# Masking the Gram matrices of a delta-rule attention on VectorE, straight out of PSUM, in a kernel for one Trainium2 core

## The chip, the cores and the metric

The kernel runs on one core of one Trainium2 chip. Its time is the device time of one execution in microseconds (us); the number given is the median of three runs. The engines are named as in the profile: PE (TensorE, matrix products; PEld is its loading of weights), DVE (VectorE), ACT (ScalarE), POOL (GpSimd), and SP (SyncE, which only issues DMAs here). PSUM is the memory that PE writes to; SBUF is the memory that all engines share.

## The reference

Three stages follow each other. First a delta-rule attention with batch 4, 8 heads, 768 tokens and head size 48, here per batch and head:

```
for t in range(S):
    y[t]  = q[t] @ state
    v_old = k_n[t] @ state                 # k_n: k over its norm
    state = state + beta[t] * outer(k_n[t], v[t] - v_old)
```

Its output, 3072 tokens of 384 values, goes through a mixture of 4 experts (`relu(x @ w1[e]) @ w2[e]`, 384 to 1024 to 384, weighted by normalized probabilities), and then through a gated layer (`sigmoid(x @ w_gate) * (x @ w_val) @ w_out`, 384 to 1536 to 384). All values are fp32.

## The kernel before

**Steps.** The token loop is cut into 12 steps of 64 tokens. A step handles all 32 pairs of batch and head: two halves of the batch lie on partitions 0 to 63 and 64 to 127, and an index i of 2 and 8 heads lie in the free dimension. Within a step the recurrence becomes matrix products: a Gram matrix of keys with keys gives L, which must be scaled by a weight per token (`w_all`, made of beta and the key norms) and inverted as a triangular system, and a Gram matrix of keys with queries gives P, which must be masked to be strictly triangular. From step 4 on, two steps share one inverse, and the six pairs of steps feed six blocks of 512 tokens to the two layers.

**Layers.** The layers are PE's main load. Each fp32 product is made of three fp32r products (high and low parts of both factors, `split3`). A unit of an expert has 9 matmuls up (`ph`, L689) and 9 down (`acc`, L726). Between them ScalarE writes the high part `hhi` of the activations (L696) and VectorE the low part `hlo`; the products down of a unit are emitted two units after the products up, those of the last three units of an expert one after the other. Weight tiles are split as they come: a ScalarE cast for the high part (`ws`, L190) and a VectorE subtraction for the low one. At an expert's end VectorE scales the three accumulators (`ctmp`) and GpSimd adds them to `ACC` (L753). VectorE's calls go through a counting wrapper and all show line 112 in the profile.

**Order.** It is written out by a planner when the kernel is built. `plan(t, fn, "pe")` gives a task a due time on PE's own account of work; `slot()` is called between the groups of layer matmuls and emits tasks that are due, one task with PE work at a time. Two lists of background work are filled in as VectorE's account (`vec_at`, which `vec.` calls raise) allows: the multiplies and subtractions of the inverse (`itmp`, `Xpp`, `Lpp`), and, until about 390 us, the decoding of the gated layer's weights (`dec_a`, `dec_b`, parts of `Xpp` and `Lpp` as buffers), which uses ScalarE, VectorE and two GpSimd products (L239, L240) each. Every engine runs its own list in order.

**The Gram matrices.** `plan_g` (L863) plans steps 4 to 11; steps 0 to 3 are done at the start. It loads keys and queries (`KQ`), copies keys into block-diagonal weights (`bdG`), and plans four tasks, one for each i and group of 4 heads. A task runs four matmuls into one PSUM bank `pg` (`g_mm`, L314; the profile counts eight), which holds 64 columns of L and 64 of P for each head. `g_raw` (L338) has ScalarE copy the bank to the tile `LP`. Nine units of due time after the first task, in one entry:

```
plan(t + 23, lambda: (scale_l(c), l_out(c), l_off(c), scale_p(c), p_out(c)))
```

`scale_l` (L347) and `scale_p` (L342) are GpSimd products over the whole step, 128x1024 each, in place in `LP`; `l_out` and `p_out` send L and P to DRAM by GpSimd's DMA queue (`ld`, `pd`), from where the inverse and the outputs read them back. `pg` is taken from the pool `at`, which has two banks in this part of the program and serves the attention's other tasks too.

Steps 0 and 1 do the same at the start with `g_l` (L321) and `g_p` (L330): VectorE multiplies the bank's L by the weights and its P by the mask and writes `LP`, 128x256 each.

Of the kernel before, what the change touches and what calls it, by code (L numbers as in the profile page):

```python
# [40 lines left out]
WARM0, WARM1 = 4, 14  # L41
DEC0, DEC1 = 7.0, 150.0
CH1, CH2, TR1, TR2 = 70.0, 42.0, 44.0, 16.0
# inverses: the steps that share one, and whether it stops at half chunks
INV = [((0,), True), ((1,), True), ((2, 3), True)]
INV += [((2 * k, 2 * k + 1), False) for k in range(2, NPAIR)]

# [25 lines left out]
AT2 = {k: n for n, k in enumerate(ORDER2)}  # L73
NG1, NG2 = len(ORDER1) // 2, len(ORDER2) // 2

# (kind, block, expert, first step of the block, number of steps)
EARLY = 1
PHASES = [("m1", 0, e, s, 1) for s in range(2) for e in range(EARLY)]
PHASES += [("m1", 0, e, 0, 2) for e in range(EARLY, NE)] + [("m2", 0, 0, 0, 2)]
# [5 lines left out]
def moe_delta_kernel(  # L85
# [13 lines left out]
):  # L99
    nc = tc.nc  # L100

    # what the tensor and vector engines have been given so far, in microseconds of their own work
    pe_at, vec_at = [0.0], [0.0]

    class Counted:
# [38 lines left out]
    KQi = [KQ[:, :, i] for i in range(2)]  # L144
    KS = ap_.tile([112, 2, H, C], F32, name="KS")
    bdG = ap_.tile([112, 2, H, P], F32, name="bdG")
# [15 lines left out]
    p_d = dr1.tile([NE, NT], F32, name="p_d")  # L162
    w2_d = dr1.tile([NG2, P, 2 * DM], F32, name="w2_d")

    # ------------------------------------------------------------ weights
    stream = []
    for kind, b, e, _, _ in PHASES:
        stream += [(kind, e * NG1 + g) for g in range(NG1)] if kind == "m1" else [(kind, g) for g in range(NG2)]
# [99 lines left out]
        items.sort(key=lambda r: r[0])  # L268
        back["dec"] += items

    # ------------------------------------------------------------ attention
    x_hi, x_lo = {}, {}
    x_done = set()
    ld_t, od_t, xd_t, pd_t = {}, {}, {}, {}
# [7 lines left out]
    def load_kq(c):  # L282
        (q[1] or q[0]).dma_start(out=KQ, in_=kq[c])
# [4 lines left out]
    def fill_bd(bd, t, i, eng):  # L288
        eng(out=bd[64:112, i, :, 0:C], in_=t[i][64:112, 0])
        eng(out=bd[0:48, i, :, C:P], in_=t[i][0:48, 0])  # L290
# [18 lines left out]
    def bank(shape, name):  # L309
        turn[0] += 1  # L310
        p, tag = free[turn[0] % len(free)]
        return p.tile(shape, F32, tag=tag, name=name)

    def g_mm(i, hg, bd, kq_t):  # L314
        pg = bank([P, 4, 2, C], "pg")
        for j in range(4):
            h = hg * 4 + j
            nc.tensor.matmul(out=pg[:, j], lhsT=bd[0:112, i, h], rhs=kq_t[i][0:112, :, h], start=True, stop=True)  # L318
        return pg

    def g_l(pg, c, i, hg):  # L321
        hs = slice(hg * 4, hg * 4 + 4)
        vec.tensor_tensor(
            out=Lts[c % 2][:, i, hs],
            in0=pg[:, :, 0],
            in1=w_all[:, 2 * c + i, hs].unsqueeze(2).to_broadcast([P, 4, C]),
            op=ALU.mult,
        )

    def g_p(pg, c, i, hg):  # L330
        vec.tensor_tensor(
            out=Pts[c % 2][:, i, hg * 4 : hg * 4 + 4],
            in0=pg[:, :, 1],
            in1=mask_sb.unsqueeze(1).to_broadcast([P, 4, C]),
            op=ALU.mult,
        )

    def g_raw(pg, c, i, hg):  # L338
        hs = slice(hg * 4, hg * 4 + 4)
        nc.scalar.copy(out=LP[c % 2][:, :, i, hs].rearrange("p a h t -> p h a t"), in_=pg)  # L340

    def scale_p(c):  # L342
        t = Pts[c % 2].rearrange("p i h t -> p (i h) t")
        m = mask_sb.unsqueeze(1).to_broadcast([P, 2 * H, C])
        nc.gpsimd.tensor_tensor(out=t, in0=t, in1=m, op=ALU.mult)

    def scale_l(c):  # L347
        t = Lts[c % 2].rearrange("p i h t -> p (i h) t")
        w = w_all[:, 2 * c : 2 * c + 2].rearrange("p i h -> p (i h)").unsqueeze(2).to_broadcast([P, 2 * H, C])
        nc.gpsimd.tensor_tensor(out=t, in0=t, in1=w, op=ALU.mult)  # L350

    def l_out(c):
        lt = Lts[c % 2]
        r, c2 = INV_OF[c]
        steps, small = INV[r]
        l_done.add(c)
        lv = [lt[o : o + HC].rearrange("p i h t -> p (i h) t") for o in range(0, P, HC)]
        if small:
            if c2 == 0:
                ld_t[r] = dr.tile([len(steps), 2, 2, H, 2, HC, HC], F32, tag=f"ls{len(steps)}", name="ls")  # L360
                od_t[r] = dr.tile([len(steps), 2, H, 2, HC, HC], F32, tag=f"lo{len(steps)}", name="lo")
            for a in range(2):
                for bp in range(2):
                    q[0].dma_start(
                        out=ld_t[r][c2, a, :, :, bp].rearrange("i h s t -> s (i h) t"),
                        in_=lv[2 * bp + a][:, :, a * HC : (a + 1) * HC],
                    )
            return
        if c2 == 0:
            ld_t[r] = dr.tile([len(steps), 2, H, 2, HC, 3 * HC], F32, tag="ld", name="ld")  # L370
        for bp in range(2):
            ld = ld_t[r][c2, :, :, bp]
            q[0].dma_start(out=ld[:, :, :, 0:C].rearrange("i h s t -> s (i h) t"), in_=lv[2 * bp])
            q[0].dma_start(
                out=ld[:, :, :, C:].rearrange("i h s t -> s (i h) t"), in_=lv[2 * bp + 1][:, :, HC:]
            )

    def l_off(c):
        lt = Lts[c % 2]
        r, c2 = INV_OF[c]  # L380
        if INV[r][1]:
            for bp in range(2):
                q[0].dma_start(
                    out=od_t[r][c2, :, :, bp].rearrange("i h s t -> s (i h) t"),
                    in_=lt[bp * C : bp * C + HC].rearrange("p i h t -> p (i h) t")[:, :, HC:],
                )

    def p_out(c):
        pd_t[c] = dr.tile([P, 2 * H * C], F32, tag=f"pd{c % 2}", name="pd")
        q[0].dma_start(out=pd_t[c], in_=Pts[c % 2].rearrange("p i h t -> p (i h t)"))  # L390
# [211 lines left out]
            rows += [[lambda i=i: s_task(c, i) for i in range(2)]] if c < NC - 1 else []  # L602
        return rows

    # ------------------------------------------------------------ norms
    nt_ = cp.tile([P, 3, 2 * NC, H], F32, name="norm_tmp")

    def norm_sum(t, c0, n):
# [47 lines left out]
        )  # L656
        nc.sync.dma_start(out=p_d.rearrange("e (g j) -> g e j", j=P), in_=d)

    # ------------------------------------------------------------ mixture
    acc_t, p_t = {}, {}  # L660

    def load_p(n):
# [95 lines left out]
                out=x_lo[b, 2][:, d, cols], in0=a, in1=xh.bitcast(F32), op=ALU.subtract  # L758
            )

    # ------------------------------------------------------------ schedule
    def unit_us(kind, ns):
        return (18 if kind == "m1" else 27) * (ns * STEP / 2.4e3 + 0.0025)

# [9 lines left out]
    def plan(t, fn, kind=""):  # L774
        todo.append((t, len(todo), kind, fn))
# [87 lines left out]
    def plan_g(c, t):  # L863
        plan(t, lambda: load_kq(c))
        for i in range(2):
            plan(t + 12, lambda i=i: fill_bd(bdG, KQi, i, nc.scalar.copy))
        for n, (i, hg) in enumerate([(0, 0), (0, 1), (1, 0), (1, 1)]):
            plan(t + 14 + 2 * n, lambda i=i, hg=hg: g_raw(g_mm(i, hg, bdG, KQi), c, i, hg), "pe")
        plan(t + 23, lambda: (scale_l(c), l_out(c), l_off(c), scale_p(c), p_out(c)))

    def startup():
        zero = pre_lo[:, 0]
# [145 lines left out]
    with tc.manual_schedule():  # L1018
# [11 lines left out]
        for c in range(4, NC, 2):  # L1030
            t = dec_mem[c // 2] if c < NC - 2 else dec_mem[2]
# [9 lines left out]
        for k in range(1, NPAIR):  # L1041
            w = W[k]
            if k > 1:
                r0 = max(M2[0] + 27.0, w - 270.0)
                plan_inv(k + 1, r0, r0 + 22.0, w - CH1 - 14.0)
            if k + 1 < NPAIR:
                plan_g(2 * k + 2, w - 161.0)
                plan_g(2 * k + 3, w - 135.0)
            plan_chain(2 * k, w - (CH1 if k > 1 else 70.0), 3.9)
            plan_chain(2 * k + 1, w - (CH2 if k > 1 else 34.0), 3.9)  # L1050
            plan_tr(2 * k, w - (TR1 if k > 1 else 22.0), 4.0)
            plan_tr(2 * k + 1, w - (TR2 if k > 1 else 8.0), 4.0)
# [100 lines left out]
```

## Time and profile before

| | |
|---|---|
| median of 3 runs | 1531.97 us (1531.19 to 1533.07) |
| the profiled execution: its span, first to last instruction | 1529.9 us; no other time of it is given |
| PE busy | 1473.9 us (96%) |
| PEld busy | 1224.4 us (80%) |
| DVE busy | 1089.4 us (71%) |
| ACT busy | 592.7 us (39%) |
| POOL busy | 303.4 us (20%) |
| mean granted PE clock | 0.978 of full speed |

The shares are means over stages with different limits. Up to about 100 us PE starts up; from 150 to 300 us VectorE is busy nearly all the time; from 300 us on PE is. Matmuls are pipelined, so the duration of a single one in a row (about 390 ns for 128x512) overlaps with the next. In rows of waits the engine on the left stood idle for the one on the right, and "idle before" belongs to the instruction behind it. The granted clock is a share of PE's full speed; 0.5 is its lower level, 1.2 GHz.

### The profile page before, as it was taken

How to read it: one execution, taken by the hardware profiler on the slowest of the kernel's cores; microseconds unless marked ns; L12 is line 12 of the kernel's file. 1: busy time of each engine (PE TensorE's matmuls, PEld its weight loads, DVE VectorE, ACT ScalarE, POOL GpSimd, SP SyncE). 2: the span in 40 equal slices, each digit the busy share in tenths (PEclk: the TensorE clock that was granted, in tenths of full speed). 3: DMA queues.
4: the chain of work that ended last, by engine and by line, in shares of the span. 5: the costliest groups of instructions: out<-in, count | busy, mean ns of one | idle time of the engine just before them, and what ended most of it. 6: DMA issues, size and time to landing. Idle time of an engine off the chain costs nothing. (4 is left out here: it accounts for less than half of the span.)

```text
span 1529.9 us, 23026 instructions
## 1 busy us (share of the span) xinstructions
PE 1473.9 (96%) x8801; PEld 1224.4 (80%) x8801; DVE 1089.4 (71%) x1841; ACT 592.7 (39%) x953; POOL 303.4 (20%) x309
## 2 busy tenths in 40 slices
PE   5899989999999999999999999999999999999998
PEld 5688767888887888887888887788888888888877
DVE  7877998846889866778756778766778754444553
ACT  4045554533343334344343444343433333433343
POOL 4241567530033210013210003220001120001100
PEclk8689999999999999999999999999999999999999
DMA  8586776675443584434485334494433462433221
GB/s 227 165 262 208 225 244 238 213 210 157 147 138 107 164 202 142 131 121 147 134 222 156 122 121 131 132 236 142 142 100 106 124 167 84 133 108 101 93 93 62
DMA packets 97749, 235.50 MB, mean 154 GB/s; under 512 B 23544, under 2 KB 29816, under 8 KB 95608
## 3 DMA queue, kind: packets, MB, share of 16 engines
q1 hardware_dynamic: 87352, 195.04, 41.2%
q0 software_dynamic: 10144, 38.94, 9.7%
q8 instruction: 69, 1.13, 0.3%
q14 instruction: 40, 0.33, 0.1%
q10 hardware_dynamic: 144, 0.07, 0.0%
HBM read 202.10 MB, written 27.97 MB: 150 GB/s over the span
## 5 line engine op out<-in xcount | busy, mean ns | idle before, releaser
L689 PE MATMUL ph<-xhi,ws 128*128 128x512 f32 (+1 forms) x2064 | 635.7, 390 | 1.5 <-ACT xhi L756 0.8
L726 PE MATMUL acc<-hhi,ws 128*128 128x512 f32 (+1 forms) x1632 | 499.0, 388 | 1.3 <-ACT hhi L696 1.3
L689 PEld LDWEIGHTS ph<-xhi,ws 128*128 128x128 f32 x2064 | 378.8, 189 | 77.1 <-ACT xhi L589 1.3
L689 PE MATMUL ph<-xlo,ws 128*128 128x512 f32 (+1 forms) x1032 | 398.2, 386 | 0.7 <-DVE xlo L112 0.6
L112 DVE TENSOR_TENSOR ws<-raw,ws 128x768 fp32r<-128x768 f32 x308 | 316.0, 1028 | 81.6 <-ACT ws L190 78.9
L726 PEld LDWEIGHTS acc<-hhi,ws 128*128 128x128 f32 x1632 | 303.1, 190 | 60.7 <-ACT hhi L696 1.7
L726 PE MATMUL acc<-hlo,ws 128*128 128x512 f32 (+1 forms) x816 | 316.7, 388 | 21.4 <-DVE hlo L112 21.4
L190 ACT CAST ws<-raw 128x768 fp32r<-128x768 f32 x308 | 254.0, 830 | 89.1 <-PE acc L726 70.0
L696 ACT ACTIVATE hhi<-ph 128x512 fp32r<-128x512 f32 (+1 forms) x200 | 116.2, 581 | 382.2 <-PE ph L689 374.5
L689 PEld LDWEIGHTS ph<-xlo,ws 128*128 128x128 f32 x1032 | 194.4, 188 | 41.8 <-DVE xlo L112 2.4
L112 DVE SCALAR_TENSOR_TENSOR hlo<-ph,hhi 128x512 fp32r<-128x512 f32 (+1 forms) x200 | 132.4, 666 | 117.8 <-ACT hhi L696 117.7
L726 PEld LDWEIGHTS acc<-hlo,ws 128*128 128x128 f32 x816 | 154.7, 190 | 57.6 <-DVE hlo L112 27.2
L112 DVE TENSOR_TENSOR itmp<-Xpp,Lpp 128x120 f32<-128x120 f32 (+27 forms) x403 | 189.5, 482 | 9.6 <-DMA Lpp<-ls 3.4
L112 DVE TENSOR_TENSOR Xpp<-Xpp,itmp 128x120 f32<-128x120 f32 (+27 forms) x403 | 185.9, 473 | 5.3
L112 DVE TENSOR_TENSOR gv<-ph,sg 128x512 f32<-128x512 f32 x72 | 49.7, 691 | 94.7 <-PE ph L689 94.6
L753 POOL TENSOR_TENSOR ACC<-ACC,ctmp 128x512 f32<-128x512 f32 x36 | 51.2, 1434 | 306.2 <-DVE ctmp L112 306.1
L705 ACT CAST hhi<-gv 128x512 fp32r<-128x512 f32 x72 | 44.6, 620 | 171.9 <-DVE gv L112 171.9
L350 POOL TENSOR_TENSOR LP<-LP,w_all 128x1024 f32<-128x1024 f32 x10 | 20.3, 2032 | 334.6 <-ACT LP L340 327.4
L112 DVE TENSOR_TENSOR hlo<-gv,hhi 128x512 fp32r<-128x512 f32 x72 | 51.3, 713 | 49.4 <-ACT hhi L705 49.4
L703 ACT ACTIVATE sg<-ph 128x512 f32<-128x512 f32 x72 | 43.0, 597 | 76.9 <-PE ph L689 76.9
L318 PE MATMUL pg<-KQ,bdG 112*128 112x128 f32 x320 | 45.0, 291 | 14.5 <-ACT bdG L290 11.4
L318 PEld LDWEIGHTS pg<-KQ,bdG 112*128 112x128 f32 x320 | 43.7, 205 | 19.1 <-ACT bdG L290 13.0
(163 smaller groups left out, 1125.0 us busy)
## 6 DMA issues: line engine op xcount, KB each, us to landing
raw<-in_wp SPq DMA_DIRECT2D x200, 384.0 KB, 3.0
raw<-w_d SPq DMA_DIRECT2D x108, 384.0 KB, 3.3
KQ<-in_kq SPq DMA_DIRECT2D x9, 896.0 KB, 8.4
pd<-LP POOLq DMA_DIRECT2D x12, 512.0 KB, 5.5
YQ<-pd POOLq DMA_DIRECT2D x24, 256.0 KB, 7.0
Lpp<-ld POOLq DMA_DIRECT2D x8, 768.0 KB, 12.6
pe<-p_d SPq DMA_DIRECT2D x23, 256.0 KB, 4.4
dec_a<-in_wp SPq DMA_DIRECT2D x15, 384.0 KB, 4.3
```

The costliest lines, as they stand in the source:

```text
L112: return fn(*args, **kw)
L190: nc.scalar.copy(out=w[:, 0], in_=t)
L318: nc.tensor.matmul(out=pg[:, j], lhsT=bd[0:112, i, h], rhs=kq_t[i][0:112, :, h], start=True, stop=True)
L350: nc.gpsimd.tensor_tensor(out=t, in0=t, in1=w, op=ALU.mult)
L689: nc.tensor.matmul(out=res[q], lhsT=lt, rhs=rt, start=(k == 0 and j == 0), stop=(k == KT - 1 and j == 2))
L696: nc.scalar.activation(out=hh, in_=res[0], func=AF.Relu)
L703: nc.scalar.activation(out=sg, in_=res[0], func=AF.Sigmoid)
L705: nc.scalar.copy(out=hh, in_=gv)
L726: nc.tensor.matmul(out=acc_t[d][:, :w], lhsT=lt, rhs=rt, start=(u == 0 and j == 0), stop=(u == nf - 1 and j == 2),)
L753: (nc.vector if e == NE - 1 else nc.gpsimd).tensor_tensor(out=a, in0=a, in1=t, op=ALU.add)
```

## The change

For steps 4 to 11 a Gram task now ends with `g_l` and `g_p` in place of the ScalarE copy, and the entry that sends L and P off has no GpSimd products any more:

```
+        def g_task(i, hg):
+            pg = g_mm(i, hg, bdG, KQi)
+            g_l(pg, c, i, hg)
+            g_p(pg, c, i, hg)
+
         for n, (i, hg) in enumerate([(0, 0), (0, 1), (1, 0), (1, 1)]):
-            plan(t + 14 + 2 * n, lambda i=i, hg=hg: g_raw(g_mm(i, hg, bdG, KQi), c, i, hg), "pe")
-        plan(t + 23, lambda: (scale_l(c), l_out(c), l_off(c), scale_p(c), p_out(c)))
+            plan(t + 14 + 2 * n, lambda i=i, hg=hg: g_task(i, hg), "pe")
+        plan(t + 23, lambda: (l_out(c), l_off(c), p_out(c)))
```

Steps 0 to 3 stay as they are. The other lines of the diff take away comments. Since `g_l` and `g_p` are counted calls, they raise VectorE's account in the planner; the order of PE and of SyncE comes out the same.

On VectorE, in step 6, the order around the tasks reads as follows; `LP_117` is the tile that takes L and P of even steps, `itmp` and `Xpp` belong to the inverse, `ws` and `hlo` to the layers.

```order
 L112 SCALAR_TENSOR_TENSOR hlo<-ph,hhi 128x512
 L112 TENSOR_TENSOR Xpp<-Xpp,itmp 128x17x31
+L112 TENSOR_TENSOR LP_117<-pg,w_all 128x256
+L112 TENSOR_TENSOR LP_117<-pg,mask_sb 128x256
 L112 TENSOR_TENSOR itmp<-Xpp,Lpp 128x510
+L112 TENSOR_TENSOR LP_117<-pg,w_all 128x256
+L112 TENSOR_TENSOR LP_117<-pg,mask_sb 128x256
 L112 TENSOR_TENSOR ws<-raw,ws 128x768
 L112 SCALAR_TENSOR_TENSOR hlo<-ph,hhi 128x512
```

The pairs of products are inserted between the inverse's instructions, and nothing else moves.

Step 4 has the one place on VectorE where background work is moved, at the third and fourth task; `dec_a`, `dec_b` and `Lpp` are buffers of the decoding there.

```order
+L112 TENSOR_TENSOR LP_117<-pg,w_all 128x256
+L112 TENSOR_TENSOR LP_117<-pg,mask_sb 128x256
 L112 TENSOR_SCALAR Lpp<-Xpp 128x384
+L112 TENSOR_TENSOR itmp<-Xpp,Lpp 128x247
 L112 TENSOR_SCALAR dec_a<-dec_a 128x384
 L112 SCALAR_TENSOR_TENSOR dec_b<-dec_b,dec_a 128x384
-L112 TENSOR_TENSOR itmp<-Xpp,Lpp 128x247
 L112 TENSOR_SCALAR dec_a<-dec_b 128x384
+L112 TENSOR_TENSOR LP_117<-pg,w_all 128x256
+L112 TENSOR_TENSOR LP_117<-pg,mask_sb 128x256
 L112 TENSOR_TENSOR ws<-raw,ws 128x768
 L112 SCALAR_TENSOR_TENSOR hlo<-ph,hhi 128x512
```

One multiply of the inverse stands two places earlier, and all four products of these tasks come before the split and the hlo.

On GpSimd, behind the tasks of step 4, its two products on `LP_117` go; the DMAs that send L (`ld`) and P (`pd`) stay.

```order
 L240 TENSOR_TENSOR dec_b<-dec_b,dec_a 128x384
-L350 TENSOR_TENSOR LP_117<-LP_117,w_all 128x1024
-L373 DMA ld<-LP_117 32x16x64
-L374 DMA ld<-LP_117 32x16x32
-L373 DMA ld<-LP_117 32x16x64
-L374 DMA ld<-LP_117 32x16x32
-L345 TENSOR_TENSOR LP_117<-LP_117,mask_sb 128x1024
+L373 DMA ld<-LP_117 32x16x64
+L374 DMA ld<-LP_117 32x16x32
+L373 DMA ld<-LP_117 32x16x64
+L374 DMA ld<-LP_117 32x16x32
 L390 DMA pd<-LP_117 128x1024
```

The DMAs keep their order and now follow the decode product directly.

## Rows read from the trace of the kernel before

**Rows 1.** The page, busy us, share of the span, instructions

```profile
PE 1473.9 (96%) x8801; PEld 1224.4 (80%) x8801; DVE 1089.4 (71%) x1841; ACT 592.7 (39%) x953; POOL 303.4 (20%) x309
```

**Rows 2.** PE's waits, 160 to 250 us: us in total, times, longest

```profile
PE acc L726 <- DVE hlo L112: 10.7, 4, 4.9
```

**Rows 3.** PE's waits, 400 to 1000 us

```profile
PE acc L726 <- DVE hlo L112: 9.1, 9, 1.7
```

**Rows 4.** Timeline of PE: start, us, instruction, [idle before <- releaser]

```profile
184.77 0.50 PE L726 MATMUL acc<-hlo,ws 128*128 128x512 f32 x1 [2.53 <-DVE hlo L112]
200.86 0.61 PE L726 MATMUL acc<-hlo,ws 128*128 128x512 f32 x1 [4.88 <-DVE hlo L112]
...
232.85 0.80 PE L726 MATMUL acc<-hlo,ws 128*128 128x512 f32 x1 [2.85 <-DVE hlo L112]
...
448.04 0.50 PE L726 MATMUL acc<-hlo,ws 128*128 128x512 f32 x1 [0.20 <-DVE hlo L112]
460.94 0.50 PE L726 MATMUL acc<-hlo,ws 128*128 128x512 f32 x1 [1.72 <-DVE hlo L112]
488.18 0.50 PE L726 MATMUL acc<-hlo,ws 128*128 128x512 f32 x1 [1.30 <-DVE hlo L112]
```

**Rows 5.** Timeline of VectorE, splits of weight tiles about step 6

```profile
439.42 0.96 DVE L112 TENSOR_TENSOR ws<-raw,ws 128x768 fp32r<-128x768 f32 x1 [2.48 <-ACT ws L190]
...
445.36 2.03 DVE L112 TENSOR_TENSOR ws<-raw,ws 128x768 fp32r<-128x768 f32 x1 [1.83 <-ACT ws L190]
...
448.50 4.27 DVE L112 TENSOR_TENSOR ws<-raw,ws 128x768 fp32r<-128x768 f32 x1
```

**Rows 6.** Timeline of GpSimd, mask product of step 6

```profile
449.54 2.40 POOL L345 TENSOR_TENSOR LP<-LP,mask_sb 128x1024 f32<-128x1024 f32 x1
```

**Rows 7.** Instructions on LP, 160 to 1000 us: count, ns min/median/max, first and last start

```profile
L340 ACT COPY LP<-pg x32: 567/587/592, 169.7 to 952.2; 128x512 f32<-128x512 f32 x32
...
L350 POOL TENSOR_TENSOR LP<-LP,w_all x8: 1895/2016/2070, 185.9 to 952.9; 128x1024 f32<-128x1024 f32 x8
L345 POOL TENSOR_TENSOR LP<-LP,mask_sb x8: 2377/2406/2416, 190.9 to 957.9; 128x1024 f32<-128x1024 f32 x8
```

**Rows 8.** Timeline, a decode product on GpSimd and an hlo on VectorE

```profile
226.03 1.42 POOL L239 TENSOR_TENSOR dec_b<-dec_b 128x384 f32<-128x384 f32 x1 [0.35 <-issue]
...
226.68 0.68 DVE L112 SCALAR_TENSOR_TENSOR hlo<-ph,hhi 128x512 fp32r<-128x512 f32 x1
```

**Rows 9.** Timeline of VectorE at the start, products of step 1

```profile
21.21 0.41 DVE L112 TENSOR_TENSOR LP<-pg,mask_sb 128x256 f32<-128x256 f32 x1
21.54 0.41 DVE L112 TENSOR_TENSOR LP<-pg,w_all 128x256 f32<-128x256 f32 x1
```

**Rows 10.** Timeline, VectorE and PE in steps 4 and 5

```profile
169.23 0.41 DVE L112 TENSOR_TENSOR Xpp<-Xpp,itmp 128x252 f32<-128x252 f32 x1
...
213.78 0.28 DVE L112 TENSOR_TENSOR Xpp<-Xpp,itmp 128x135 f32<-128x135 f32 x1
...
214.36 1.05 PE L318 MATMUL pg<-KQ,bdG 112*128 112x128 f32 x8
```

**Rows 11.** Stretches: us, busy PE PEld DVE ACT POOL, clock, DMA share, GB/s

```profile
168.00:185.00 17.00, 14.47 (x80) 12.21 (x79) 16.86 (x32) 10.90 (x20) 8.46 (x8) 1.00 0.53 172
185.00:201.00 16.00, 11.12 (x49) 8.84 (x49) 15.96 (x15) 5.83 (x10) 13.85 (x13) 1.00 0.81 257
201.00:233.00 32.00, 27.84 (x129) 22.54 (x129) 31.45 (x55) 16.98 (x31) 19.66 (x21) 0.93 0.81 255
434.00:446.00 12.00, 12.00 (x70) 10.47 (x69) 7.19 (x11) 5.02 (x9) 1.33 (x1) 1.00 0.20 66
```

**Rows 12.** Stretches, PE alone: us, busy, granted clock, DMA share, GB/s

```profile
184.00:190.00 6.00, 5.23 (x23) 1.00 0.98 280
200.00:206.00 6.00, 5.14 (x16) 0.72 0.36 104
231.00:240.00 9.00, 7.15 (x20) 0.62 0.76 252
```

## The prediction

> **What bounds the kernel now.** I read the shares of busy time first: TensorE (PE) works 1473.9 us, 96% of the span of 1529.9 us [rows 1], so time can only come from its 56 us of idle time or from the clock. Next come PE's waits by stretch. From 160 to 250 us, where the Gram matrices of steps 4 and 5 are built, PE stands 10.7 us for hlo, the low part of the hidden activations that VectorE writes [rows 2]. From 400 to 1000 us, where steps 6 to 11 have theirs, it stands nine times for the same tile, 9.1 us in all [rows 3]; three of these times belong to each pair of steps. The timeline gives the places: the waits of steps 4 and 5 (184.77, 200.86, 232.85) and, as the sample for the other pairs, the three of steps 6 and 7 (448.04, 460.94, 488.18) [rows 4].
>
> Why is hlo late there? VectorE's instructions beside GpSimd's two products of a step are stretched. The split of a weight tile (ws), which takes 0.96 us alone at 439.42, takes 2.03 us at 445.36 and 4.27 us at 448.50 [rows 5]; the mask product ran from 449.54 to 451.94 [rows 6]. Over the free split that is 1.07 + 3.31 = 4.4 us for this step, as much as the two products last (2.0 and 2.4 us [rows 7]). VectorE therefore stands still while GpSimd multiplies. An instruction that reads PSUM does not: hlo at 226.68 takes its usual 0.68 us inside a GpSimd product that runs from 226.03 to 227.45 [rows 8].
>
> **The change part by part.** From step 4 on there are 8 steps of 4 head groups, 32 tasks.
>
> *Removed on ScalarE:* 32 copies of 0.587 us [rows 7], 18.8 us. PE waits for VectorE at these places and not for ScalarE, so I count nothing directly. But the copies wait for PE, and the cast of the next weights is queued behind them: VectorE's split at 439.42 had stood idle 2.48 us for that cast [rows 5]. This cover goes as well, and VectorE can use the gap.
>
> *Removed on GpSimd:* 16 products, 8 x (2.0 + 2.4) = 35.2 us [rows 7]. GpSimd itself has idle time; what counts is that VectorE gets back about 4.4 us in each step.
>
> *Added on VectorE:* 64 products of 128x256 out of PSUM. The same two instructions run at the start on steps 0 and 1: 0.41 us each, and back to back one begins 0.33 us after the other (21.21 and 21.54) [rows 9]. A step gets 8 of them: 8 x 0.33 = 2.6 us, in all 21.1 us. They read PSUM, so rows 8 say that GpSimd does not stretch them; some will run while GpSimd blocks VectorE's other work anyway, and cost less. The other end of the price is the sum of their full durations, 3.3 us a step.
>
> *Moved:* hardly anything. PE and SyncE keep their order. On VectorE the products are put in where the tasks stand, and one multiply of the inverse moves up by two places. On GpSimd the DMAs of L and P (ld, pd) follow the decode products directly; they wait for VectorE instead of ScalarE, and behind them stand the expert sums (ACC). VectorE delivers P before GpSimd's old second product would have ended, so pd leaves earlier.
>
> *The new wait:* PE's third group of a step needs the bank that the first group's products free, since these tasks share two banks. In steps 6 to 11 VectorE is close behind PE. In step 5 it is not: the first products stand in front of the multiply that began at 213.78, and would end at 213.78 + 0.33 + 0.41 = 214.5, while the third group's matmuls began at 214.36 [rows 10]. I count up to 0.5 us.
>
> *Steps 6 to 11.* From 434 to 446 us VectorE works only 7.19 of 12.00 us [rows 11]: the 2.6 us of step 6 go into its idle time. The 4.4 us given back come between 445 and 453, ahead of the hlo that PE waits 1.72 us for at 460.94. GpSimd's three ACC sums, which stretch VectorE too, move earlier, and this doesn't eat them up: VectorE must wait for PE's accumulators there, and gains perhaps 1.2 us at first, but then its multiplies are no longer squeezed between the sums. In step 7 the queue is fuller: 2.6 us come in, 4.4 us go out, and both old product times lie ahead of 488.18, so hlo is 1.8 us earlier there against a wait of 1.30 us. All nine waits should go: 9.1 us.
>
> *Steps 4 and 5.* From 168 to 201 us VectorE works 16.86 of 17.00 and 15.96 of 16.00 us [rows 11], so every added product is late work. Step 4 puts 2.6 us in front of the wait at 184.77; with a little of it hidden under the decode products I take 2.0, so that wait grows from 2.53 to 4.5 us. By 200.86 VectorE has 4.4 us back and PE is 2 us later: the 4.88 us there go. 2.53 + 4.88 = 7.4 becomes 4.5: gain 2.9. In step 5, 2.6 us come in before 232.85, and only the first product's 2.0 us come back before it; the bank wait takes up to 0.5, and the mask product's 2.4 us come back too late for that wait but help the one behind it. I count zero for step 5.
>
> *The clock.* After the wait at 200.86 the granted clock is 0.72 on average from 200 to 206 us, and about the wait at 232.85 it is 0.62 from 231 to 240 [rows 12]: for a part of each stretch PE runs at the lower level, 1.2 GHz, after standing. From 184 to 190, behind the wait of 2.53 us, it is 1.00 [rows 12]. That is 6 x 0.28 = 1.7 and 9 x 0.38 = 3.4 us of full speed lost. If the wait at 200.86 goes and the one at 184.77 grows to 4.5, nearer to the 4.88 that was followed by the low level than to 2.53, the dip only moves. I take zero, and keep 5.1 us of gain and 1.7 of loss as its ends.
>
> The Trainium skill, in "Perfetto Trace Analysis", section "Optimizing Scalar/DVE Operations", puts VectorE's cost per instruction at about 60 ns on SBUF and 125 ns on PSUM, which speaks against many small products out of PSUM. The trace does not show that difference: the product of 256 columns out of PSUM takes 0.41 us [rows 9], and a subtraction of 252 columns between SBUF tiles takes 0.41 us as well [rows 10]. By the rule the 64 products would cost 64 x 65 = 4.2 us more than SBUF ones, about 1 us of it in steps 4 and 5 where it is not covered, and the forecast would be 1521.
>
> **Sum.** Against the profiled execution, whose span is 1529.9 us: 9.1 + 2.9 = 12.0 us less, 1517.9. The median of the three runs, 1531.97, stands 2.1 us above that span; I leave this difference as it is: 1531.97 - 12.0 = 1520.0 us. After 1000 us PE has nothing to wait for but the chain that both kernels share, so what is gained stays.
>
> **Rivals.**
>
> A. *Only steps 6 to 11 gain.* In steps 4 and 5 VectorE has no idle time, decode products on GpSimd block it as soon as the Gram products no longer do, and PE waits for banks. For it: 31.45 of 32.00 us busy from 201 to 233 [rows 11]. Against it: 4.4 us given back per step exceed 2.6. With a loss of up to 3 us there: 1523 to 1526.
>
> B. *The clock comes too.* The waits of step 4 shrink below what brings the low level, and those of step 5 as well: 9.1 + 2.9 and up to 5.1 more, plus up to 2.85 us of step 5's wait [rows 4]: 1512 to 1515. For it: part of the products can run while GpSimd blocks other work. Against it: step 5's wait gets more products ahead of it than time back.
>
> C. *VectorE becomes the bound, slower than before.* The time given back is taken at once by GpSimd's next work, which moves up by 4.4 us and blocks VectorE as long. Then each step adds its 2.6 us at steps 4, 5, 7, 9 and 11, of which I take half as covered in the last three: 5.2 + 3.9 = 9.1 us, and bank waits of up to 1 us: about 1542. It decides from the point where less than 2.6 of the 4.4 us come back. For it: behind the mask product three ACC sums, and in steps 4 and 5 decode products, do follow. Against it: they follow in both kernels and add nothing. The same section of the Trainium skill advises that work may be taken off a saturated VectorE, even to GpSimd, and by that the move onto it should cost; it adds that the two share a port, so that it might not help. Rows 5 agree with the second half.
>
> D. *The time comes back later.* The nine waits are replaced by waits for weights or casts at the same places. ScalarE loses work there, so I see little for it: within 3 us, 1529 to 1535.
>
> **How the numbers follow.** The forecast (1516 to 1523) has 0.55, A 0.22, B 0.13, C 0.05, D 0.05. About 0.2%, 3 us, is what a measurement of this kernel can tell from no change. Faster takes the forecast, A and B: 0.90; same 0.05; slower 0.05. The range leaves out the end of B and C and D: 1512 to 1527.
>
> **What the profile of the changed kernel would show.** Right: no GpSimd instruction on LP but DMAs, splits (ws) of 0.95 us where 2.03 and 4.27 stood; 64 products of about 0.42 us; no wait of PE for hlo from 400 to 1000 us; the wait near 185 longer, the one near 200 gone, PE's waits for hlo from 160 to 250 us near 8 us instead of 10.7. Wrong: PE waiting for pg banks on VectorE more than 1 us in all, hlo waits that stay near 461 and 488, products stretched beyond 0.5 us, or ACC sums that stretch the multiplies behind them as long as before.

## The result, and the profile after

| | before | after |
|---|---|---|
| median of the runs on the same chip | 1532.52 us (1531.19 to 1534.92, 4 runs) | 1516.91 us (1512.61 to 1520.26, 4 runs) |
| the profiled execution: its span | 1529.9 us | 1510.8 us (its own time 1512.61 us) |
| mean granted PE clock of the profile | 0.978 | 0.981 |

The ratio is 0.9897, with a 95% interval of 0.9876 to 0.9918: faster by 1.0%, 3.1 us below the forecast of 1520.0.

The page's line of busy time shows the same matmuls as [rows 1], 64 products more on VectorE, and yet 22.5 us less of VectorE's time (1089.4 before).

```profile
PE 1468.1 (97%) x8801; PEld 1222.8 (81%) x8801; DVE 1066.9 (71%) x1905; ACT 574.4 (38%) x921; POOL 264.9 (18%) x293
```

Next the instructions on `LP` after 160 us: count, duration in ns (min/median/max), first and last start. They answer to [rows 7].

```profile
L112 DVE TENSOR_TENSOR LP<-pg,w_all x32: 410/419/425, 171.5 to 935.7; 128x256 f32<-128x256 f32 x32
L112 DVE TENSOR_TENSOR LP<-pg,mask_sb x32: 407/415/421, 171.9 to 936.0; 128x256 f32<-128x256 f32 x32
L373 POOL DMA_DIRECT2D ld<-LP x16: 648/660/726, 185.7 to 937.7; - x16
```

No copy and no GpSimd product is left, only DMAs, and no product of the 64 is stretched: 425 ns is the longest.

VectorE's splits of weight tiles about step 6, in the timeline of the kernel after, answer to [rows 5]:

```profile
431.31 0.95 DVE L112 TENSOR_TENSOR ws<-raw,ws 128x768 fp32r<-128x768 f32 x1
437.24 0.95 DVE L112 TENSOR_TENSOR ws<-raw,ws 128x768 fp32r<-128x768 f32 x1
440.46 0.95 DVE L112 TENSOR_TENSOR ws<-raw,ws 128x768 fp32r<-128x768 f32 x1
```

Where 2.03 and 4.27 us stood, all take 0.95. Before the change PE had one wait from 160 to 250 us beside those of [rows 2], for the high part of the activations:

```profile
PE acc L726 <- ACT hhi L696: 1.3, 1, 1.3
```

After it, PE's waits in that stretch are these (total, times, longest); from 400 to 1000 us there are none, against [rows 3].

```profile
PE acc L726 <- DVE hlo L112: 6.5, 2, 4.3
PE pg L318 <- DVE LP L112: 1.4, 2, 0.7
```

Their places in the timeline of PE, answering to the upper part of [rows 4]:

```profile
185.55 0.50 PE L726 MATMUL acc<-hlo,ws 128*128 128x512 f32 x1 [4.25 <-DVE hlo L112]
...
228.59 0.50 PE L726 MATMUL acc<-hlo,ws 128*128 128x512 f32 x1 [2.24 <-DVE hlo L112]
```

The first wait grew from 2.53 to 4.25 us, the one at 200.86 is gone, the one at 232.85 shrank from 2.85 to 2.24.

**PE's lead by stretch.** PE executes 8801 matmuls in both kernels, in one order, so the start of the same matmul in two traces tells how far one kernel is ahead. The table takes the matmuls that begin at 160, 260, 400 and 1000 us in the kernel before, in each run's profiled execution; a stretch shows what PE gained (minus) or lost in it. The startup, to 160 us, lies ahead of step 4's Gram tasks. Each row is one profile: the two of the kernel after (the first two rows) differ by 0.9 us from 160 to 260 and by 0.3 us from 400 to 1000, so smaller differences between rows tell nothing. In e9 alone PE's order is another from 168 to 322 us, and its second and third column hold different work; their sum can be compared.

| kernel, us | startup | 160-260 | 260-400 | 400-1000 | rest | without startup |
|---|---|---|---|---|---|---|
| after | -0.9 | -6.3 | -0.1 | -11.4 | -0.2 | -18.1 |
| after, once more (e6) | +5.4 | -5.4 | -0.1 | -11.7 | 0.0 | -17.3 |
| steps 6 to 11 alone (e1) | -0.1 | -0.1 | -0.2 | -11.7 | -0.2 | -12.2 |
| steps 4 and 5 alone (e2) | +0.2 | -5.8 | +0.5 | -0.1 | +0.1 | -5.3 |
| no products at all (e3) | -0.2 | -6.9 | +0.4 | -11.7 | +0.1 | -18.2 |
| both kinds of products (e4) | -0.7 | +2.2 | -0.1 | +2.9 | 0.0 | +5.0 |
| copies and VectorE products (e5) | +3.3 | +0.7 | -0.1 | -11.8 | -0.2 | -11.3 |
| decode to 165 (e7) | +0.6 | -9.2 | +11.5 | -11.7 | -0.2 | -9.6 |
| decode to 180 (e8) | +1.7 | -12.1 | +20.2 | -11.7 | -0.1 | -3.6 |
| Gram tasks later (e9) | +1.3 | -2.7 | +7.3 | -11.5 | +0.4 | -6.5 |
| inverse to 100 (e10) | +4.2 | -6.6 | +1.5 | -11.7 | -0.2 | -17.1 |
| decode sums on VectorE (e11) | +1.5 | -10.1 | +17.7 | -11.6 | -0.1 | -4.1 |
| 20 of 36 of them (e12) | +2.6 | -0.1 | +0.1 | -11.8 | 0.0 | -11.8 |

### The profile page after: what moved, and what is told of

Read it like the earlier page. It is cut to its first block, busy times and chain, and to the rows that moved or that the text cites. A ratio compares the mean times of both kernels' runs of the same rounds, so it can differ in the third digit from the quotient of the medians.

```text
span 1510.8 us, 23046 instructions
## 1 busy us (share of the span) xinstructions
PE 1468.1 (97%) x8801; PEld 1222.8 (81%) x8801; DVE 1066.9 (71%) x1905; ACT 574.4 (38%) x921; POOL 264.9 (18%) x293
## 4 chain that ended last, share of the span: by engine, by line
PE 86%; DVE 8%; DMA 3%; issue 2%; ACT 1%; SPq 0%; DVEq 0%; ACTq 0%
PE ph L689 43%; PE acc L726 33%; PE pu L521 3%; PE pg L318 2%; DVE Xpp L112 1%; DVE itmp L112 1%; PE pk L499 1%; PE ps L571 1%; DMA raw<-in_wp 1%; DVE ws L112 1%; DMA ls<-LP 1%; PE yt L534 1%; DVE hlo L112 1%; PE pu L512 1%; PE yt L535 1%
## 5 line engine op out<-in xcount | busy, mean ns | idle before, releaser
L112 DVE TENSOR_TENSOR ws<-raw,ws 128x768 fp32r<-128x768 f32 x308 | 298.3, 970 | 60.8 <-ACT ws L190 58.1
L112 DVE TENSOR_TENSOR itmp<-Xpp,Lpp 128x120 f32<-128x120 f32 (+27 forms) x403 | 174.3, 445 | 9.7 <-DMA Lpp<-ls 3.8
L112 DVE TENSOR_TENSOR Xpp<-Xpp,itmp 128x120 f32<-128x120 f32 (+27 forms) x403 | 176.2, 449 | 5.1
L373 POOL DMA_DIRECT2D ld<-LP x16 | 10.7, 670 | 333.5 <-DVE LP L112 333.5
```

Source lines behind the costliest of these rows:

```text
L112: return fn(*args, **kw)
```

## The experiments

### The change in two halves, without products, and with both kinds

*e1*: the change for steps 6 to 11 alone, the old way for 4 and 5 (e2 is the same with `c < 6`). The entry that sends L and P off is split in the same way, which is left out here:

```
-            plan(t + 14 + 2 * n, lambda i=i, hg=hg: g_task(i, hg), "pe")
+            if c >= 6:
+                plan(t + 14 + 2 * n, lambda i=i, hg=hg: g_task(i, hg), "pe")
+            else:
+                plan(t + 14 + 2 * n, lambda i=i, hg=hg: g_raw(g_mm(i, hg, bdG, KQi), c, i, hg), "pe")
```

> Only steps 6 to 11 take the change; steps 4 and 5 keep the ScalarE copies and the two GpSimd products. If the gain is each wait for hlo that goes, plus about 0.27 us after each (the trace of the change shows the 128x512 matmuls behind a wait 0.2 to 0.4 us further ahead than the wait's row says), the nine waits give 9.1 + 2.4 = 11.5 us: about 1521 us, and the waits at 185, 201 and 233 stay as before with the low clock behind them. Rival, that most of the gain is the clock in steps 4 and 5: less than 6 us, above 1526.

Measured: 1519.88 us (4 runs), ratio 0.9917 (0.9889 to 0.9945). The nine waits are gone; 160 to 260 us is as before.

*e2*:

> Only steps 4 and 5 take the change. Waits 12.0 to 7.9 us and a shorter stretch at the low clock: 4 to 7 us, 1525 to 1528 us, with nine waits for hlo left between 400 and 1000 us. If its runs fall into two groups some 6 us apart while those of the version with steps 6 to 11 alone do not, the scatter of the changed kernel's times (1512.6 to 1520.3) comes from steps 4 and 5.

Measured: 1527.13 us (7 runs), ratio 0.9956 (0.9943 to 0.9969). PE's waits from 400 to 1000 us are back to 8.9 us in nine. The seven times lie between 1525.99 and 1530.18 us and form no two groups 6 us apart, while one of e1's four lies 6 us above its others, so nothing points at steps 4 and 5 as the source of the scatter. The halves add up: 12.2 + 5.3 = 17.5 us without the startup, the whole change 17.3 and 18.1.

*e3*: the kernel before, copies and all, without GpSimd's products.

```
-        plan(t + 23, lambda: (scale_l(c), l_out(c), l_off(c), scale_p(c), p_out(c)))
+        plan(t + 23, lambda: (l_out(c), l_off(c), p_out(c)))
```

> The kernel before with its ScalarE copies, but without the 16 GpSimd products and without VectorE ones in their place: from step 4 on L is not weighted and P not masked. If GpSimd's products hold VectorE up, the nine waits go as in the changed kernel, and steps 4 and 5 get 4.4 us per step back with nothing added: 1508 to 1513 us, below the changed kernel. Rival, that the copies in ScalarE's queue delay the casts and with them hlo: the nine waits stay in most part, 1525 to 1531 us.

Measured: 1517.35 us (4 runs), ratio 0.9891 (0.9865 to 0.9917). No wait of PE from 400 to 1000 us. With the 32 copies in place the nine waits go, so they came from GpSimd's products and not from the copies. The expected 1508 to 1513 us were missed: the kernel after, with 64 products more on VectorE, is only 0.6 us (160 to 260) and 0.3 us (400 to 1000) behind e3, which is within the spread of two profiles of one kernel. In steps 6 to 11 the products therefore cost nothing that can be seen. In steps 4 and 5 they do: e3's waits from 160 to 250 us are 5.4 us against 7.9.

```profile
PE acc L726 <- DVE hlo L112: 3.7, 2, 2.5
PE acc L726 <- ACT hhi L696: 1.1, 1, 1.1
PE acc L726 <- DVE ws L112: 0.6, 1, 0.6
```

These 2.5 us don't show in the time, because e3 ran at the lower clock once more, about its waits at 222 to 226 us. This row of PE (busy and count, granted clock, DMA share, GB/s) stands against 1.00 from 226 to 240 us in the kernel after:

```profile
226.00:240.00 14.00, 13.74 (x48) 0.79 0.69 243
```

That is 14 x 0.21 = 2.9 us of full speed. So the added products cost 2.5 us of waits, and a difference of clock hides them.

*e4*: the kernel after with GpSimd's two products kept as well; L is weighted twice.

```
-        plan(t + 23, lambda: (l_out(c), l_off(c), p_out(c)))
+        plan(t + 23, lambda: (scale_l(c), l_out(c), l_off(c), scale_p(c), p_out(c)))
```

> The changed kernel with the 16 GpSimd products put back behind it, so L is weighted twice from step 4 on (P masked twice is P). VectorE has the 64 products and is held up as before. If the hold-up is what counts, the waits at 461 and 488 and their like come back and grow, by up to 2.6 us in steps 7, 9 and 11, and steps 4 and 5 pay 2.6 us each: 1533 to 1545 us. Rival, that the gain came from the ScalarE copies: it stays, near 1517.

Measured: 1540.44 us (6 runs), ratio 1.0044 (1.0026 to 1.0061). PE's waits from 400 to 1000 us:

```profile
PE acc L726 <- DVE hlo L112: 10.2, 6, 2.0
```

The split of weights beside GpSimd's mask product of step 6 is stretched again, in the timeline of VectorE:

```profile
449.75 4.27 DVE L112 TENSOR_TENSOR ws<-raw,ws 128x768 fp32r<-128x768 f32 x1
```

The difference between e4 and the kernel after is GpSimd's work alone, and it is 23.1 us without the startup (5.0 + 18.1): these products cost PE time by holding VectorE, as waits, and as lower clock about some of them (0.83 from 490 to 500 us, behind a wait of 2.01 us). Against the kernel before, e4 loses 5.0 us without the startup and 6.4 us in the medians (1540.44 against 1534.01 on the same chip). Rival C had 10.1 us for a time that isn't given back, so its price was one and a half to two times too high; its 1542 lies near e4's 1540 partly because the kernel before took 2 us more on that chip.

### Does it matter that the products read PSUM?

*e5*: ScalarE copies, VectorE multiplies in SBUF.

```
         def g_task(i, hg):
             pg = g_mm(i, hg, bdG, KQi)
-            g_l(pg, c, i, hg)
-            g_p(pg, c, i, hg)
+            g_raw(pg, c, i, hg)
+            ... (the views l and p of LP, and w and m)
+            vec.tensor_tensor(out=l, in0=l, in1=w, op=ALU.mult)
+            vec.tensor_tensor(out=p, in0=p, in1=m, op=ALU.mult)
```

> The changed kernel with the ScalarE copies put back: each Gram task of steps 4 to 11 is copied out of PSUM by ScalarE (0.59 us each, two per task), and the two VectorE products then read and write SBUF. GpSimd's products stay gone. Theory (the nine waits came from GpSimd products holding VectorE): the nine hlo waits of 400 to 1000 us stay away and PE starts 15 us or more earlier at the end than in the kernel before; 1514 to 1520 us, within 3 us of the changed kernel. Rival (the copies in ScalarE's queue, and the PSUM bank they hold, were the cause): at least half of the nine waits comes back, 1521 to 1526 us. On the side: if VectorE reads SBUF cheaper than PSUM, the product takes under 0.40 us instead of 0.41; beside GpSimd's decode sums in steps 4 and 5 a product with two SBUF operands is stretched to over 0.6 us, which the products out of PSUM were not.

Measured: 1523.74 us (4 runs), ratio 0.9938 (0.9923 to 0.9953). This hits neither theory: from 400 to 1000 us the waits stay away, 11.8 us gained as in the kernel after, and from 160 to 260 us all of that stretch's gain is lost. The median lies in the rival's range, but its sign, the nine waits, is missing. Two rows of e5 in step 4, GpSimd's decode sum and the first product of VectorE:

```profile
175.64 1.10 POOL L240 TENSOR_TENSOR Xpp<-Xpp,dec_b 128x384 f32<-128x384 f32 x1
...
175.77 1.25 DVE L112 TENSOR_TENSOR LP<-LP,w_all 128x256 f32<-128x256 f32 x1
```

The product begins 0.13 us after the sum and lasts until 0.28 us after the sum's end; alone it takes 0.41. Five of the 16 products of steps 4 and 5 take 1.05 to 1.52 us. VectorE's products from 160 to 250 us, by their busy time (us, busy and count, clock, DMA share, GB/s), first after, then e5:

```profile
160.00:250.00 90.00, 5.97 (x16) 0.98 0.75 241
```

```profile
160.00:250.00 90.00, 10.04 (x16) 0.92 0.72 229
```

So in steps 4 and 5, where GpSimd's decode sums run, the same 16 products cost 4.1 us more with both operands in SBUF. The Trainium skill, in "SBUF — State Buffer", section "SBUF: two separate sides", has it that a VectorE instruction with two SBUF inputs and a GpSimd instruction that reads SBUF exclude each other: the one that starts first has the shared ports for its whole length. These rows agree, 1.25 us against 0.41, and [rows 8] show the other side of it. What the copies add in steps 4 and 5 together with the products was not separated; copies without products (e3) gain 6.9 us there.

### Where the two groups of times come from

*e6*: the kernel after, nothing edited.

> The changed kernel once more, nothing edited: its four times stood at 1512.6, 1513.9, 1519.9 and 1520.3 us. If the gap of 6 to 7 us is made by TensorE's clock, the profiled run, where it is a long one, shows 10 us or more of additional low-clock stretches beside those at 108 and 186 us, and the same waits. If it is made by something else (DMA arrival at the start), the low-clock stretches are the same and the first matmul behind the startup starts 5 us or more later. Median expected 1517 us, between 1513 and 1520.

Measured: 1517.91 us (5 runs, 1513.1 to 1519.78), ratio 0.9892 (0.9872 to 0.9912). The profiled execution was the longest, 1519.78 us, with a span of 1518.0, 7.2 us over that of the first profile. The matmul of the first wait, in e6:

```profile
191.88 0.79 PE L726 MATMUL acc<-hlo,ws 128*128 128x512 f32 x1 [4.26 <-DVE hlo L112]
```

The wait is the same, 4.26 and 4.25 us, and stands 6.3 us later than in the kernel after (185.55). These 6.3 us arise in the startup; from there on the two differ by under 1 us. PE from 100 to 130 us (busy and count, granted clock, DMA share, GB/s), first after, then e6:

```profile
100.00:130.00 30.00, 26.44 (x270) 0.83 0.81 264
```

```profile
100.00:130.00 30.00, 25.95 (x232) 0.72 0.74 234
```

In these 30 us the longer one has done 38 matmuls less at a lower granted clock, and it falls back by 3.7 us (the lead changes from +1.7 to +5.4 us between 100 and 145 us); the other 2.6 us arise before 100 us. The clock isn't all of the 3.7. In the timeline of PE one wait of that stretch is 1.7 us longer, first after, then e6:

```profile
106.73 2.75 PE L521 MATMUL pu<-R,Xbd 128*128 128x48 f32 x16 [2.32 <-DVE R L112]
```

```profile
111.04 3.65 PE L521 MATMUL pu<-R,Xbd 128*128 128x48 f32 x16 [4.05 <-DVE R L112]
```

VectorE's R stands there behind the norms of keys, and ScalarE's square for the norms waits for a transfer, 0.16 us in the kernel after and 2.45 us in e6:

```profile
95.78 1.48 ACT L1039 ACTIVATE dec_a<-dec_a 128x1536 f32<-128x1536 f32 x1 [0.16 <-DMA dec_a<-in_kt]
```

```profile
100.64 1.48 ACT L1039 ACTIVATE dec_a<-dec_a 128x1536 f32<-128x1536 f32 x1 [2.45 <-DMA dec_a<-in_kt]
```

So both signs of my expectation came, low clock and late arrival by DMA. It was seen in two profiles; which of the two comes first was not tried.

### Can the waits that stay be thinned out?

VectorE is full from 150 to 300 us, with the decode, the inverse and the products. Each of these kernels moves one of the three on the base of the kernel after.

*e7, e8*: the decode spread over more of the plan (e8 with 180.0).

```
-DEC0, DEC1 = 7.0, 150.0
+DEC0, DEC1 = 7.0, 165.0
```

> The changed kernel with the 36 decode items of the gated layer spread over 158 us of the plan instead of 143 (end of the plan at 165 for 150), so that steps 4 and 5 hold a tenth fewer of them. Theory (in steps 4 and 5 VectorE is full: 28.4 of 30 us, 26.6 of 30 and 27.2 of 30, and the hlo waits of 4.25 and 2.24 us are what does not fit): the two waits together fall from 6.5 to about 4 us; 1512 to 1516 us. Rival (the waits are set by the order in which the products stand ahead of hlo, not by the load): the waits stay within 1 us, 1515 to 1519 us.

> As the one with the plan's end at 165, but at 180: 173 us for 143, steps 4 and 5 hold a sixth fewer decode items, and the last of them move to 305 to 335 us, where VectorE is busy for 14.8 of 30 us. Theory (VectorE is full in steps 4 and 5): the two hlo waits fall from 6.5 to 2 us or less, and if the clock follows the waits the low-clock stretch behind 185 us goes as well (1.7 us); 1508 to 1513 us. Rival (order, not load): waits within 1 us of 6.5, 1515 to 1519 us. Rival (the clock does not follow the waits): waits gone, but low-clock stretches of 3.4 us or more stay in 180 to 240 us, 1512 to 1515 us.

Measured: e7 1521.94 us (4 runs), ratio 0.9928 (0.9908 to 0.9948); e8 1532.22 us (10 runs), ratio 0.9998 (0.9985 to 1.0011). The load theory holds where it was asked: 160 to 260 us gains 9.2 and 12.1 us instead of 6.3, and the hlo waits fall from 6.5 to 4.1 and 2.9 us. The time is lost behind: 11.5 and 20.2 us from 260 to 400. In e7, PE and VectorE there:

```profile
339.97 2.79 PE L512 MATMUL pu<-R,Xbd 128*96 128x48 f32 x16 [6.54 <-DVE R L112]
```

```profile
338.49 0.96 DVE L112 TENSOR_TENSOR ws<-raw,ws 128x768 fp32r<-128x768 f32 x1 [8.82 <-ACT ws L190]
339.37 0.55 DVE L112 TENSOR_TENSOR R<-V,pk 128x384 f32<-128x384 f32 x1
```

VectorE stands for a cast of gated-layer weights, and R is queued behind. The chain of waits of that stretch names the transfer of the decoded weights first:

```profile
by line: DMA raw<-w_d 23.6%; PE ph L689 18.5%; issue 15.1%; PE pu L512 10.3%; ACT ws L190 5.0%; PE acc L726 4.5%; DVE Xpp L112 4.3%; DVE gv L112 4.0%; DVE dec_b L112 3.7%; DVE ws L112 2.3%; ACT hhi L705 1.6%; PE ps L571 1.5%; DVE Lpp L112 1
```

The decode has a reader with a date of its own, the gated layer, which neither of my expectations had named. The decoding ends earlier than I had said ahead of the prediction (about 390 us): the last GpSimd product on `dec_a` (L239) begins at 319.9 us in the kernel before and at 312.6 us in the kernel after. Both medians lie above the expected ranges.

*e9*: the Gram tasks of steps 4 and 5, 47 us later.

```
+                d = 47.0 if k == 1 else 0.0
-                plan_g(2 * k + 2, w - 161.0)
-                plan_g(2 * k + 3, w - 135.0)
+                plan_g(2 * k + 2, w - 161.0 + d)
+                plan_g(2 * k + 3, w - 135.0 + d)
```

> The changed kernel with the Gram tasks of steps 4 and 5 planned 47 us later (from about 171 and 200 us of the span to about 225 and 255), where the inverse of steps 2 and 3 no longer runs beside them; steps 6 to 11 stay. Theory (the waits left in steps 4 and 5 come from a VectorE that has the inverse, the decode and the products at once): PE's waits of 160 to 250 us fall from 8 to 4 us or less (3.7 us is what stays without any products), the low-clock stretch behind 186 us goes or shrinks, and behind the startup PE stands 21 to 24 us ahead of the kernel before instead of 18; 1510 to 1515 us. Rival (the load only moves, as with the decode items that were spread): the same 5 to 8 us of waits appear at 225 to 300 us, 1515 to 1521 us.

Measured: 1525.31 us (6 runs), ratio 0.9948 (0.9933 to 0.9963). From 160 to 400 us together e9 loses 4.6 us where the kernel after gains 6.5. The two columns for themselves tell less: up to the mark of 260 us e9 has done 32 matmuls of the layers more (0.23 us apart in its timeline) and 32 of Gram tasks fewer (0.11 us apart), by my estimate 3.6 us of work brought forward. PE's waits from 160 to 250 us are 5.9 us, not 4 or less, and 6.2 us of waits appear from 260 to 300 us: the rival, and its time was worse than it said.

*e10*: the inverse of steps 2 and 3 spread to 100 in place of 80.

```
-LOUT, INV2 = 4.0, (8.0, 14.0, 80.0)
+LOUT, INV2 = 4.0, (8.0, 14.0, 100.0)
```

> The changed kernel with the inverse of steps 2 and 3 spread over 86 us of the plan instead of 66 (its end at 100 for 80), so that VectorE has about a quarter fewer of its itmp and Xpp products per us between 160 and 226 us, and has the rest between 226 and 246. Theory as for the later Gram tasks: waits of 160 to 250 us fall from 8 to 5 us, 1512 to 1516 us. Rival (the load only moves): 1515 to 1522 us, with waits for hlo or R behind 226 us.

Measured: 1519.12 us (4 runs), ratio 0.9907 (0.9887 to 0.9926). Its profiled startup was 4.2 us late; without it 17.1 us are gained, no more than by the kernel after. The hlo waits from 160 to 250 us stay at 6.8 us, all waits of PE there at 8.4 us, so the theory fell. Its interval overlaps that of the kernel after.

*e11*: GpSimd's product and sum of each decode item on VectorE; e12 the same for the first 20 of 36 items, and not counted in the planner's account.

```
-            nc.gpsimd.tensor_tensor(out=lf, in0=lf, in1=hf, op=ALU.mult)
-            nc.gpsimd.tensor_tensor(out=t, in0=t, in1=lf, op=ALU.add)
+            vec.tensor_tensor(out=lf, in0=lf, in1=hf, op=ALU.mult)
+            vec.tensor_tensor(out=t, in0=t, in1=lf, op=ALU.add)
```

> The changed kernel with the two GpSimd operations of each of the 36 decode items (a product and a sum of 128x384, about 1 us each) put on VectorE. Theory (a GpSimd operation on SBUF holds VectorE for about the time that it takes from it): between 146 and 306 us VectorE's operations stand 29 us above the shortest time of their kind, 0.8 us for each item; two more 128x384 operations of VectorE cost about 0.45 us of pitch each, 0.9 an item. So VectorE's load comes out level, and the time too: 1512 to 1521 us, with no VectorE operation at more than 1.3 times its shortest time in 230 to 300 us. Rival (GpSimd's work is free beside VectorE): 33 us more on a full VectorE, 1530 us or more.

> The changed kernel with the two GpSimd operations of the first 20 of 36 decode items (to about 228 us of the span) on VectorE, in the places where GpSimd's were issued; nothing else moves. With all 36 moved, and the plan counting them, PE stood 10.8 us ahead of the kernel before at 260 us (counted from the end of the startup; the changed kernel 6.3), but lost 17 us at 300 to 400, where the decode came to lie. Theory (a GpSimd operation costs VectorE about what it saves it, only in lumps): the load stays level, the lumps go, PE's waits of 160 to 250 us fall from 8 to 4 to 6 us, those of 250 to 400 stay at 0.6 us; 1511 to 1517 us. Rival (the gain at 260 us was decode put off, not lumps): waits of 160 to 250 us stay at 7 to 10 us, 1516 to 1521 us.

Measured: e11 1524.92 us (4 runs), ratio 0.9945 (0.9925 to 0.9965); e12 1521.87 us (6 runs), ratio 0.9928 (0.9905 to 0.9950). In e11 the plan put the decode off, with the loss of e7 and e8 behind (17.7 us), and its time hit neither range. In e12 nothing else moved, and 160 to 260 us has lost all of its 6.3 us. VectorE's load did come out level, even a little lower, as its busy time from 160 to 260 us shows (busy and count, clock, DMA share, GB/s), first after, then e12:

```profile
160.00:260.00 100.00, 92.44 (x164) 0.98 0.75 242
```

```profile
160.00:260.00 100.00, 89.67 (x190) 0.95 0.72 235
```

What fell is that PE's waits follow this load. The rival that the gain of e11 was only decode put off stands, though both its numbers were too low (7 to 10 us of waits, up to 1521 us); why the waits grew with a level load is open. Of the 6.2 us that e12 is behind the kernel after there, 3.4 are waits (8.1 for hlo, 1.6 for ws, 1.6 for banks: 11.3 against 7.9), and the granted clock is 0.92 from 210 to 240 us against 1.00. The Trainium skill, in "Perfetto Trace Analysis", section "Optimizing Scalar/DVE Operations", holds that moving work between VectorE and GpSimd might not help. The runs here have both outcomes: the decode sums are better left on GpSimd, by 6 us (e12), and the Gram products better on VectorE, by 18 us.

None of these beats the kernel after; e10 can't be told from it.

## Why the prediction was right, step by step

**VectorE stands still while GpSimd multiplies: right, and shown.** Taking the products away alone gives the gain (e3), keeping them beside the new ones gives it back with a loss (e4), and the splits take 0.95 us. The 4.4 us that I set against the two products agree as a sum only: the first product of step 6 cost its split 1.07 us, because VectorE stood idle for a cast as the product began, and the mask product of 2.40 us cost 3.31. Why it cost 0.9 us more than it lasts is open.

**Products out of PSUM are not stretched, 0.41 us each: right.** All 64 lie between 407 and 425 ns; from SBUF, beside the decode sums, five of 16 take 1.05 us or more (e5). The sentence on PSUM and SBUF at 60 and 125 ns would have made 1 us of difference; products with SBUF operands take the same where GpSimd doesn't multiply, as e5 has them from 400 to 1000 us:

```profile
L112 DVE TENSOR_TENSOR LP<-LP,w_all x24: 415/419/427, 440.1 to 946.7; 128x256 f32<-128x256 f32 x24
```

**Copies counted at nothing: right for steps 6 to 11.** e3 keeps them and gains as much there.

**Steps 6 to 11, 9.1 us: the mechanism right, the term too small.** All nine waits went, and PE gained 11.4 us there in the kernel after, 11.7 in e1 and e3. The missing 2.3 us are in how a wait is read. The timeline of PE about the second of them, before:

```profile
458.61 0.61 PE L726 MATMUL acc<-hhi,ws 128*128 128x512 f32 x2
460.94 0.50 PE L726 MATMUL acc<-hlo,ws 128*128 128x512 f32 x1 [1.72 <-DVE hlo L112]
461.28 0.63 PE L726 MATMUL acc<-hhi,ws 128*128 128x512 f32 x2
```

The same matmuls after:

```profile
450.68 0.61 PE L726 MATMUL acc<-hhi,ws 128*128 128x512 f32 x2
451.13 0.39 PE L726 MATMUL acc<-hlo,ws 128*128 128x512 f32 x1
451.36 0.61 PE L726 MATMUL acc<-hhi,ws 128*128 128x512 f32 x2
```

From the first row to the third it is 2.67 us before and 0.68 after: 1.99 us for a row that says 1.72. The row counts from the modelled end of the matmul ahead, which lasts 0.39 us though the next begins after 0.23; that hides 0.16 us, and the first matmul behind the wait delays the next by 0.34 instead of 0.23, another 0.11. Nine times 0.27 is 2.4 us. I had the 0.50 of that matmul in my rows and summed only the brackets. One sign against me, ACC sums that stretch VectorE's multiplies as long as before, came in half: of two multiplies beside them in step 6, which took 1.67 and 1.68 us, one still takes 1.66 and the other 0.69.

**Step 4, from 2.53 to 4.5 us, and the wait at 200.86 gone: right.** 4.25 us, and gone. Without any products (e3) the wait stays at 2.53 us, so step 4's products cost it 1.7 us where I had 2.0.

**Step 5 counted at zero: partly wrong.** The wait for hlo fell from 2.85 to 2.24 us. The banks took 1.4 us instead of up to 0.5, more than the 1 us that I had named as a sign against me: I had followed the third group's bank alone, and the fourth waits for the second group's as well, 0.7 us each.

**The clock counted at zero: the term that was mis-sized in steps 4 and 5.** The waits there fell by 4.1 us (10.7 and a wait for hhi of 1.3 to 6.5 and 1.4; 2.9 predicted), and PE gained 6.3. Three stretches of PE in the kernel before (columns as in [rows 12]):

```profile
184.00:194.00 10.00, 9.23 (x40) 1.00 0.97 278
200.00:210.00 10.00, 9.14 (x36) 0.83 0.48 159
226.00:240.00 14.00, 9.84 (x31) 0.76 0.86 309
```

and in the kernel after:

```profile
184.00:194.00 10.00, 8.45 (x30) 0.83 0.91 301
200.00:210.00 10.00, 10.00 (x52) 1.00 0.52 179
226.00:240.00 14.00, 11.65 (x51) 1.00 0.83 292
```

The dip behind 200 us moved to behind 185, as forecast, and the one about 232 us, 14 x 0.24 = 3.4 us of full speed, went altogether. This is the second half of rival B. About 2 of the 3.4 us show in PE's lead; in the rest of that dip PE stood anyway.

**The sum.** Profile against profile it is 19.1 us: 0.9 of the startup, 6.3, 11.4, and 0.4 in the two other stretches. I had 2.9 and 9.1, without the clock and without the 0.27 us of each wait. In the medians it is 15.6 us, nearer to the forecast, because two of the four times of the kernel after lie over 7 us above the profiled one, as e6's profiled time does for its startup: that part of the agreement is luck.

**The rivals.** A is out (steps 4 and 5 gained). B came in half. C's condition didn't occur, and its price was one and a half to two times what a kernel loses that keeps GpSimd's products (e4). D is out: PE has no wait from 400 to 1000 us.

## What to carry to other kernels

Where VectorE sets the end of PE's waits, look at what GpSimd does at that moment before counting VectorE's own work: here 35 us of GpSimd products were worth 18 us of the end, and 64 more VectorE instructions out of PSUM cost 2.5 us of PE's waits, all in the two steps where VectorE was full. Add to every wait of PE that goes what the row leaves out around it, here 0.27 us, and look at the granted clock behind it. Where a stage is full because several things are spread over it, find the reader behind one of them before spreading it further: here the stage itself became faster by up to 6 us, and the gated layer behind it lost more (e7, e8).

## What the runs showed of the hardware that was not expected

A wait of the same length was followed by different clocks: behind one of 2.53 us the granted clock from 184 to 194 us was 1.00 in the kernel before, while in e1, behind one of 2.52 us, it was this:

```profile
184.00:194.00 10.00, 9.35 (x35) 0.83 0.97 274
```

In e10 a wait of 2.90 us, to 189.37, was followed by this:

```profile
189.00:199.00 10.00, 9.63 (x42) 1.00 0.95 293
```

The kernel after itself shows it, too: behind the same wait of 4.25 us the clock was 0.83 from 184 to 194 us in its first profile, and in e6, behind 4.26 us, it was this:

```profile
190.00:200.00 10.00, 8.12 (x24) 0.66 0.94 290
```

So the dips can't be read off the length of the wait alone, and a gain of a dip, about 2 us here, can't be promised beforehand.
